# The routing's small tiles in a PSUM bank, and the output rows' positions worked out one step per half step

## The chip, the cores and the metric

The kernel runs on one core of one Trainium2 chip. The metric is the device time of one execution in microseconds; lower is better. Before the change the median of three runs is 992.59 us (992.57 to 993.57). A core has five engines with queues of their own, each served in order: TensorE (PE, its weight loads PEld), VectorE (DVE), ScalarE (ACT), GpSimd (POOL) and SyncE (SP), which here only issues DMAs. SBUF is the memory that all of them reach, PSUM the memory of eight banks that TensorE writes and that VectorE and ScalarE read and write.

## The reference, cut to what matters

Three parts follow each other: an attention with a threshold, a mixture of experts with one expert per token, and a dense layer with a gate. The kernel computes all three in one launch.

```python
scores = scale * q @ k.T; scores = where(scores >= max - tau, scores, -1e9)
x = softmax(scores) @ v                       # 4 x 8 heads x 576 x 64 -> 2304 tokens x 512
logits = x @ w_gate + modality_bias[modality_id]
e_idx = argmax(logits, 1); gate_w = softmax(logits)[e_idx]
for e in range(8):                            # each token through its own expert
    out[e_idx == e] = gate_w * (relu(x[e_idx == e] @ w1[e]) @ w2[e])
h = out @ w_in                                # 512 -> 2048
y = (h * tanh(softplus(h))) @ w_out           # 2048 -> 512
```

## The kernel before, in words

**Attention** goes over 16 pairs of heads in 80 units, TensorE scoring, VectorE and ScalarE masking and exponentiating. When the tokens of a batch are done, `gate` computes their logits and the chosen expert as a one-hot tile `oh`. After half of the tokens, `route_a` (L780) finds the largest expert and gathers the rows of the first item, so that the expert stage can start before the routing is done.

**The expert stage** works in items of 512 rows (`W`) that belong to one expert: five in the straight part (NST), the last one of 288 rows. An item has 8 steps (NF), one for each 128 columns of the hidden layer; n counts the steps over all items, 40 in all. Step n loads the weights of step n + 2 (`load_step`, SP queue), splits weights into a high and a low half (`w_split`, ScalarE and GpSimd, L937 and L938, tiles w0h, w0l, w1h, w1l), runs the up pass of 12 matmuls, splits its relu into hh (ScalarE, L956) and hl (VectorE, L957), and runs the down pass of step n - 1, which needs the hh and hl of that step. From n = 9 (DEC0) on VectorE also decodes the weights of the dense layer (`dec_bits`, L1172 to L1176, a PSUM tile `dect`), one chunk a step and two at some steps (DECB); their loads `dr` (L1164) are issued on the SP queue.

**The routing** proper, `route_b` (L806), runs beside the first item. It is a list of some 90 small steps, nearly all VectorE instructions on tiles of 1 to 240 columns: `ops(1)` (L674) ranks the tokens of the second half within their experts; the lines L826 to L866 compute the experts and the starts of the items (registers `regs`); `place(0)` (L815, L817 to L820) gives every token a position in the items, and `Ids` (L703) turns positions into a list of row numbers `ids_p`, by comparing (at, L735; one-hots qt, L724), marking (ab, L729) and four groups of five small matmuls (L769) whose sum ScalarE copies to `lo` (L775) and VectorE combines (L753). With `ids_p` GpSimd gathers the rows of the second item (`gather_all`, indirect DMAs, L882), which TensorE turns (`x_turn`, L898, eight transposes to a pair of tiles). After that, `rd` does the same for the positions in the output (`place(1)` and a second `Ids`, to `ids_d`), which only the dense layer's stores use, from 688 us on.

**What sets the order.** The engines' queues are written out by the program. `run_bg` (L1205) is called in `half`, twice a step, once before and once after the down pass (h = 2n and 2n + 1). It takes steps off the list `bg` while a planned clock stays below a limit: a small step is planned at 0.19 us (DVC), a step of `Ids` at 0.06 us and more. Pieces with a `pe` part (the small matmuls) are put into TensorE's queue when the plan says that their operands are ready. When `bg` is empty, `half` issues the gather and appends `rd()` to `bg`:

```python
if 1 not in xg and not bg:
    run_pool(99)
    xg[1] = gather_all(ids_p[:, 0:4], xg_p)
    xs[1] = x_new()
    turn_at = next(i for i in range(2 * NF) if i == 2 * NF - 2 or pe_time(i) > clock[0] + DVG)
    bg.extend(rd())
```

At the end of step 8 the list must be empty; the pools of the routing are closed and the first three loads of `dr` issued into their place. All routing tiles lie in SBUF. PSUM is split into two pairs of banks (`ps_s`), a ring of three banks (`ps_t`, `pt_tile`) and one single bank (`ps_a`, `pa_tile`), which attention uses for its results, `x_turn` for every second tile of the second item's rows, and decoding for `dect`.

**The dense layer** follows, with TensorE and VectorE both near full.

Of the kernel before, what the change touches and what calls it, by code (L numbers as in the profile page):

```python
# [25 lines left out]
E = 8  # L26
# [60 lines left out]
def chain_kernel(ctx: ExitStack, tc: tile.TileContext, q, k, v, tau, mid, w_gate, mbias, w1, w2, w_in, w_out, cst, out):  # L87
# [564 lines left out]
    one = C("ones")[:, 0:E * HC]  # L652
# [8 lines left out]
    class Totals(Piece):  # L661
# [8 lines left out]
        def ev(self):  # L670
            nc.scalar.copy(out=pre[self.h], in_=self.t)


    def ops(h, pl):  # L674

        o = oh[:, h]
        of = o.rearrange("p e c -> p (e c)")
        exc, tmp = f("exc", E, HC, pl=pl), f("tmp", E, HC, pl=pl)
        ds, dp, pb = f("ds", HC, pl=pl), f("dp", 2, pl=pl), f("pb", E, pl=pl)
        t2 = f("t2", 2, E, pl=pl)  # L680
        wb = wsw.unsqueeze(2).to_broadcast([P, E, HC])
        excf = exc.rearrange("p e c -> p (e c)")
        return [

            lambda: vec.tensor_tensor(out=t2, in0=pre[h], in1=wsw.unsqueeze(1).to_broadcast([P, 2, E]), op=ALU.mult),
            lambda: vec.tensor_tensor(out=tmp, in0=o, in1=wb, op=ALU.mult),
            lambda: vec.tensor_reduce(out=dp, in_=t2, op=ALU.add, axis=AX.X),
            lambda: vec.tensor_reduce(out=ds, in_=tmp.rearrange("p e c -> p c e"), op=ALU.add, axis=AX.X),
            lambda: vec.tensor_tensor(out=t2, in0=dp.unsqueeze(2).to_broadcast([P, 2, E]),
                                      in1=wsw.unsqueeze(1).to_broadcast([P, 2, E]), op=ALU.mult),  # L690
            lambda: vec.tensor_tensor(out=tmp, in0=ds.unsqueeze(1).to_broadcast([P, E, HC]), in1=wb, op=ALU.mult),
            lambda: vec.tensor_tensor(out=pre[h], in0=pre[h], in1=t2, op=ALU.subtract),
            lambda: vec.tensor_tensor(out=o, in0=o, in1=tmp, op=ALU.subtract),
            lambda: vec.tensor_tensor_scan(out=excf, data0=one, data1=of, initial=0.0, op0=ALU.mult, op1=ALU.add),
            lambda: vec.tensor_tensor(out=exc, in0=exc, in1=o, op=ALU.subtract),
            lambda: vec.tensor_tensor(out=pb, in0=pre[h][:, 0, :], in1=exc[:, :, 0], op=ALU.subtract),
        ] + ([lambda: vec.tensor_tensor(out=pb, in0=pb, in1=pre[0][:, 1, :], op=ALU.add)] if h else []) + [
            lambda: vec.tensor_tensor(out=exc, in0=exc, in1=pb.unsqueeze(2).to_broadcast([P, E, HC]), op=ALU.add),
            lambda: vec.tensor_tensor(out=exc, in0=exc, in1=o, op=ALU.mult),
            lambda: vec.tensor_reduce(out=rank[:, h], in_=exc.rearrange("p e c -> p c e"), op=ALU.add, axis=AX.X),  # L700
        ]

    class Ids:  # L703


        def __init__(self, pos, nc_, nb, ids, pl):
            self.a = (pos, nc_, nb, ids)
            self.pi, self.ai = f("pi", nc_, dt=I32, pl=pl), f("ai", nc_, dt=I32, pl=pl)
            self.af, self.qf = f("af", nc_, pl=pl), f("qf", nc_, pl=pl)
            m, self.qc = (1, HC) if nc_ == HC else (2, HC // 2)  # L710
            self.at = f("at", self.qc, nb, dt=BF16, pl=pl)
            self.ab = [f(f"ab{i}", self.qc, 2, nb, dt=BF16, pl=pl) for i in range(m)]
            self.qt = [f(f"qt{i}", self.qc, P, dt=BF16, pl=pl) for i in range(m)]
            self.lo = f("lo", 2, nb, pl=pl)

        def some(self, c0):
# [4 lines left out]
            qt, ab = (z[c0 // qc % 2] for z in (self.qt, self.ab))  # L721
# [34 lines left out]

    class IdSum(Piece):
# [4 lines left out]
        def pe(self):  # L762
# [4 lines left out]
            qt, ab = (z[c0 // o.qc % 2] for z in (o.qt, o.ab))  # L767
# [12 lines left out]
    def route_a(pl):  # L780
# [18 lines left out]
            *ops(0, pl),  # L799
# [3 lines left out]
            *Ids(pos0, HC, 4, ids_0, pl).steps(),  # L803
        ]

    def route_b(pl):  # L806
        tot, cmp, ni, nis, ist, start, off = (f(n, E, *([NST] if n == "cmp" else []), pl=pl)
                                              for n in ("tot", "cmp", "ni", "nis", "ist", "start", "off"))
        it_e, it_p, i16, fw = f("it_e", NIT, pl=pl), f("it_p", NIT, pl=pl), f("i16", NIT, pl=pl), f("fw", 1, pl=pl)
        it_c, it_d = f("it_c", NIT, E, pl=pl), f("it_d", NIT, E, pl=pl)  # L810
        b0, b0i, wide = f("b0", 1, pl=pl), f("b0i", 1, dt=I32, pl=pl), f("wide", 1, pl=pl)
        sel, pos = f("sel", 2, E, HC, pl=pl), f("pos", 2, 2, HC, pl=pl)
        bi = [P, NIT, E]

        def place(z, base):  # L815
# [3 lines left out]
                    lambda: vec.tensor_reduce(out=pos[:, z], in_=sel.rearrange("p h e c -> p h c e"), op=ALU.add, axis=AX.X),  # L819
                    lambda: vec.tensor_tensor(out=pos[:, z], in0=pos[:, z], in1=rank, op=ALU.add)]  # L820
# [4 lines left out]
            *ops(1, pl),  # L825
            lambda: vec.tensor_tensor(out=tot, in0=pre[0][:, 1, :], in1=pre[1][:, 1, :], op=ALU.add),  # L826
# [4 lines left out]
            lambda: vec.tensor_tensor_scan(out=nis, data0=one[:, 0:E], data1=ni, initial=0.0, op0=ALU.mult, op1=ALU.add),  # L831
            lambda: vec.tensor_tensor_scan(out=start, data0=one[:, 0:E], data1=tot, initial=0.0, op0=ALU.mult, op1=ALU.add),
# [5 lines left out]
            *place(0, ist),  # L838
            lambda: vec.tensor_scalar(out=fw, in0=full, scalar1=-float(W), scalar2=None, op0=ALU.mult),
            lambda: vec.tensor_scalar(out=pos[:, 0], in0=pos[:, 0], scalar1=fw[:, 0:1], scalar2=None, op0=ALU.add),  # L840
# [27 lines left out]
            *Ids(pos[:, 0].rearrange("p h c -> p (h c)"), NC, NBLK, ids_p, pl).steps(),  # L868
        ], lambda: [*place(1, start), *Ids(pos[:, 1].rearrange("p h c -> p (h c)"), NC, NT // P, ids_d[:, 0:NT // P], pl).steps()]
# [28 lines left out]
    def x_turn(xg, x, kd, w=W, single=True):  # L898
        t = (pa_tile("xt") if single and kd % 2 == 0 else pt_tile([P, W], "xt"))[:, 0:w]
# [492 lines left out]
    def half(h):  # L1392
# [9 lines left out]
        if 1 not in xg and not bg:  # L1402
# [4 lines left out]
            bg.extend(rd())  # L1407
# [13 lines left out]
    for n in range(NS + 1):  # L1421
# [22 lines left out]
        half(2 * n)  # L1444
        if n > 0:
# [23 lines left out]
        if 4 <= g < 4 + KD and 0 < it < NST - 1:  # L1469
            x_turn(xg[it + 1], xs[it + 1], g - 4, width(it + 1), n < DEC0)  # L1470
# [11 lines left out]
    assert dp > len(dec)  # L1482
# [111 lines left out]
```

## Time and profile before

| | |
|---|---|
| median of 3 runs | 992.59 us (992.57 to 993.57) |
| the profiled execution | 996.13 us, its span 994.3 us, mean granted clock 0.988 |
| busy: TensorE | 930.9 us (94%) |
| busy: VectorE | 815.8 us (82%) |
| busy: GpSimd | 665.5 us (67%) |
| busy: ScalarE | 519.7 us (52%) |

The span runs from the first to the last instruction of the profiled execution, and all times in the rows count from its start. The expert stage lies at about 349 to 597 us, its first item at 349 to 415, its second at 415 to 462. A row of an instruction has its start, its duration, and in brackets the idle time of its engine before it and what ended it. A duration includes time in which an instruction has started and can't go on. Matmuls are pipelined, so that their rows overlap and the spacing of their starts is their pace. The granted clock is a share of TensorE's upper level.

### The profile page before, as it was taken

The page shows a single profiled execution, that of the slowest core. Times are in us where ns is not written, and L with a number is a line of the kernel's source. Part 1 is how long each engine was busy: PE and PEld are TensorE (multiplying, and loading weights), DVE is VectorE, ACT ScalarE, POOL GpSimd, SP SyncE. Part 2 cuts the span into 40 slices and gives each one's busy share as a digit, 9 for nine tenths or more (in the row PEclk, how much of TensorE's full clock was granted, in tenths as well). Part 3 has the DMA queues.
Part 4 walks back from the last instruction along what each step waited for, and adds up shares of the span by engine and source line. Part 5 has one row for each costly group of instructions (what it writes and reads, how often), then busy time and mean ns, then how long its engine had stood idle before and what let it go on. Part 6 is the DMA issues. An engine that isn't in the chain of part 4 may idle for free. (4 is left out here: it accounts for less than half of the span.)

```text
span 994.3 us, 17630 instructions
## 1 busy us (share of the span) xinstructions
PE 930.9 (94%) x6157; PEld 783.2 (79%) x6157; DVE 815.8 (82%) x1116; ACT 519.7 (52%) x1044; POOL 665.5 (67%) x771
## 2 busy tenths in 40 slices
PE   8899989998979997899999799999999999999994
PEld 5788888788868776688887788888888888888983
DVE  5677786687957768978876579999999999999992
ACT  4577777776768732366654643434344333433341
POOL 4354564455556364577876786887887888787883
PEclk9899999999999999999999999999999999999998
DMA  7678766646567053498899849010001100000000
GB/s 173 138 176 232 190 174 154 143 116 153 136 165 171 7 181 96 134 333 264 257 323 314 292 165 335 1 43 22 22 1 43 43 1 22 11 33 1 1 32 34
DMA packets 120526, 127.47 MB, mean 128 GB/s; under 512 B 54576, under 2 KB 83504, under 8 KB 119920
## 3 DMA queue, kind: packets, MB, share of 16 engines
q1 hardware_dynamic: 117472, 116.58, 40.8%
q0 software_dynamic: 2960, 9.70, 2.9%
q8 instruction: 51, 0.84, 0.3%
q14 instruction: 43, 0.35, 0.1%
HBM read 71.66 MB, written 27.33 MB: 100 GB/s over the span
## 5 line engine op out<-in xcount | busy, mean ns | idle before, releaser
L1298 DVE RECIPROCAL v<-v 128x512 f32<-128x512 f32 (+1 forms) x73 | 241.6, 3309 | 2.5
L373 DVE TENSOR_REDUCE mn<-s 128x1 f32<-128x576 f32 x144 | 106.3, 750 | 61.4 <-PE s L362 36.0
L381 ACT ACTIVATE e<-s,mn 128x576 f32<-128x576 f32 x144 | 105.1, 741 | 88.8 <-DVE mn L373 82.3
L379 POOL TENSOR_SCALAR th<-mn,taus 128x1 f32<-128x1 f32 x140 | 40.5, 290 | 147.5 <-DVE mn L373 134.5
L1292 POOL TENSOR_TENSOR u<-u,v 128x512 f32<-128x512 f32 (+1 forms) x73 | 93.1, 1276 | 64.4 <-ACT v L1291 63.0
L391 DVE SCALAR_TENSOR_TENSOR p<-s,th,e 128x576 f32<-128x576 f32 x144 | 115.2, 815 | 21.2 <-ACT e L381 9.3
L944 PE MATMUL h<-ybh,wil 128*128 128x512 f32 (+1 forms) x320 | 117.7, 368 | 0.0
L942 PE MATMUL h<-ybh,wih 128*128 128x512 f32 (+1 forms) x320 | 117.7, 368 | 0.0
L943 PE MATMUL h<-ybl,wih 128*128 128x512 f32 (+1 forms) x320 | 117.7, 368 | 0.0
L1321 PE MATMUL o<-wo,gh 128*128 128x512 f32 x288 | 112.8, 392 | 1.9 <-ACT gh L1305 1.5
L1297 DVE TENSOR_SCALAR v<-u 128x512 f32<-128x512 f32 (+1 forms) x73 | 109.5, 1500 | 5.6 <-POOL u L1292 3.7
L1323 PE MATMUL o<-wo,gl 128*128 128x512 f32 x288 | 112.7, 391 | 0.3
L1322 PE MATMUL o<-wo,gh 128*128 128x512 f32 x288 | 112.7, 391 | 0.0
L1289 ACT ACTIVATE u<-h 128x512 f32<-128x512 f32 (+1 forms) x73 | 43.2, 592 | 128.6 <-PE h L944 126.0
L1307 POOL TENSOR_TENSOR gl<-v,gh 128x512 fp32r<-128x512 f32 (+1 forms) x73 | 105.7, 1448 | 0.3 <-ACT gh L1305 0.3
L1305 ACT CAST gh<-v 128x512 fp32r<-128x512 f32 (+1 forms) x73 | 44.9, 615 | 111.3 <-DVE v L1303 111.3
L1299 POOL TENSOR_TENSOR u<-u,v 128x512 f32<-128x512 f32 (+1 forms) x73 | 93.3, 1278 | 7.7 <-DVE v L1298 7.7
L361 PE MATMUL s<-xkh,xq 128*128 128x288 f32 x248 | 81.2, 342 | 12.1 <-DVE p L391 10.1
L429 PE MATMUL av<-pt,mv 128*64 128x128 f32 (+1 forms) x1280 | 82.8, 272 | 0.0
L938 POOL TENSOR_TENSOR w0l<-w1r,w0h 128x512 fp32r<-128x512 f32 x39 | 50.7, 1300 | 47.4 <-ACT w0h L937 34.3
L401 PE MATMUL tp<-zident,p 128*128 128x128 f32 x576 | 79.3, 275 | 0.7 <-DVE p L391 0.4
L416 ACT COPY pt<-tp 128x512 f32<-128x512 f32 x144 | 78.4, 598 | 0.4 <-PE tp L401 0.4
(251 smaller groups left out, 2337.9 us busy)
## 6 DMA issues: line engine op xcount, KB each, us to landing
w1r<-in_moe_w SPq DMA_DIRECT2D x40, 256.0 KB
w2r<-in_moe_w SPq DMA_DIRECT2D x40, 256.0 KB
xkh<-hik SPq DMA_DIRECT2D x64, 144.0 KB
xkl<-lok SPq DMA_DIRECT2D x64, 144.0 KB
dr<-in_moe_w_in SPq DMA_DIRECT2D x16, 512.0 KB
dr<-in_moe_w_out SPq DMA_DIRECT2D x16, 512.0 KB
wo<-wo_d SPq DMA_DIRECT2D x14, 512.0 KB
y_d<-zero SPq DMA_DIRECT2D x8, 576.0 KB
```

The lines of the kernel that those rows point to most:

```text
L373: nc.vector.tensor_reduce(out=mn[:, x:x + 1], in_=r["s"][:, :, 0:HK], op=ALU.min, axis=AX.XY)
L381: nc.scalar.activation(out=r["e"], in_=r["s"][:, :, 0:HK], func=AF.Exp, scale=-1.0, bias=res[i, j, 0]["mn"][:, x:x + 1])
L391: nc.vector.scalar_tensor_tensor(out=p, in0=r["s"][:, :, 0:HK], scalar=res[i, j, 0]["th"][:, x:x + 1], in1=r["e"], op0=ALU.is_le, op1=ALU. ...
L942: nc.tensor.matmul(o, lhsT=wh, rhs=xh, start=first, stop=False)
L943: nc.tensor.matmul(o, lhsT=wh, rhs=xl, start=False, stop=False)
L944: nc.tensor.matmul(o, lhsT=wl, rhs=xh, start=False, stop=last)
L1297: nc.vector.tensor_scalar(out=v_, in0=u, scalar1=WTOP, scalar2=2.0, op0=ALU.min, op1=ALU.add)
L1298: nc.vector.reciprocal(out=v_, in_=v_)
L1307: nc.gpsimd.tensor_tensor(out=l, in0=v_, in1=t.bitcast(F32), op=ALU.subtract)
L1321: nc.tensor.matmul(o, lhsT=gh[:, sl], rhs=wo[0, f_], start=f_ == 0, stop=False)
L1322: nc.tensor.matmul(o, lhsT=gh[:, sl], rhs=wo[1, f_], start=False, stop=False)
L1323: nc.tensor.matmul(o, lhsT=gl[:, sl], rhs=wo[0, f_], start=False, stop=f_ == NFO - 1)
```

## The change

The tiles of `route_b` go into the single PSUM bank, so that each VectorE operation of it has one operand, or its result, there. A class `Bank` hands out columns of that bank. `wsw` is copied there by ScalarE (`wsp`), a tile of ones is set there, intermediate tiles (tmp, exc, pb, t2, the corrected totals, pos, it_c, it_e, and of `Ids` pi, ai, af, qf, at) lie there and others stay in SBUF, so that no operation has both inputs in SBUF; `it_p` is computed twice, once for each place; `fw` moves to ScalarE; only the second half of the row sums is copied to `lo`, the first is read from PSUM. `route_a` keeps its tiles in SBUF.

`rd` is no longer appended to `bg`. Its tiles lie in SBUF in a pool of their own, its `Ids` has one group of 20 columns in place of four of 5, and `later()` takes one of its 24 steps after each half of the steps n = 10 to 21. The pools of the other routing tiles are closed at the end of step 8 as before. `x_turn` takes all its tiles from the ring of three.

```diff
+    class Bank:
+        def __init__(self, t):
+            self.t, self.n = t, 0
+        def part(self, *shape, at=None):
...
+            v = self.t[:, o:o + m]
...
         def ev(self):
             nc.scalar.copy(out=pre[self.h], in_=self.t)
+            if self.h:
+                nc.scalar.copy(out=wsp, in_=wsw)
...
+    def ops(h, pl, wsw, one, bank=None):
...
+        exs, ds, dp = f("exc", E, HC, pl=pl), f("ds", HC, pl=pl), f("dp", 2, pl=pl)
+        if bank:
+            tmp, exc, pb, t2, po = (bank.part(*z) for z in ((E, HC), (E, HC), (E,), (2, E), (2, E)))
+        else:
+            tmp, exc, pb, t2, po = f("tmp", E, HC, pl=pl), exs, f("pb", E, pl=pl), f("t2", 2, E, pl=pl), pre[h]
...
-            lambda: vec.tensor_tensor(out=pre[h], in0=pre[h], in1=t2, op=ALU.subtract),
+            lambda: vec.tensor_tensor(out=po, in0=pre[h], in1=t2, op=ALU.subtract),
...
-            lambda: vec.tensor_tensor(out=exc, in0=exc, in1=o, op=ALU.subtract),
-            lambda: vec.tensor_tensor(out=pb, in0=pre[h][:, 0, :], in1=exc[:, :, 0], op=ALU.subtract),
+            lambda: vec.tensor_tensor(out=exs, in0=exc, in1=o, op=ALU.subtract),
+            lambda: vec.tensor_tensor(out=pb, in0=po[:, 0, :], in1=exs[:, :, 0], op=ALU.subtract),
...
+            if bank:
+                self.pi, self.ai = bank.part(nc_).bitcast(I32), bank.part(nc_).bitcast(I32)
+                self.af, self.qf = bank.part(nc_, at=0), bank.part(nc_, at=nc_)
+                self.at = bank.part(qc, nb, at=2 * nc_)
...
-                lambda: vec.scalar_tensor_tensor(out=ids, in0=self.lo[:, 0, :], scalar=64.0, in1=self.lo[:, 1, :],
+                lambda: vec.scalar_tensor_tensor(out=ids, in0=self.t[:, 0:nb], scalar=64.0, in1=self.lo,
...
-                nc.scalar.copy(out=o.lo.rearrange("p a b -> p (a b)"), in_=o.t)
+                nc.scalar.copy(out=o.lo, in_=o.t[:, o.a[2]:])
...
+    def route_b(pl, late, bank):
+        nonlocal wsp
+        n0 = 200
+        wsp, one = bank.part(E, at=n0), bank.part(96, at=n0 + E)
+        block = ops(1, pl, wsp, one[:, 0:E * HC], bank)
...
+        vec.memset(one, 1.0)
+        it_c = one.rearrange("p (a b) -> p a b", b=E)
+        tot, ni, ist = (bank.part(E) for _ in range(3))
...
+        ids = Ids(pos.rearrange("p h c -> p (h c)"), NC, NBLK, ids_p, pl, HC // 2, bank)
+        ids1 = Ids(pos1.rearrange("p h c -> p (h c)"), NC, NT // P, ids_d[:, 0:NT // P], late, NC)
...
-            lambda: vec.tensor_scalar(out=fw, in0=full, scalar1=-float(W), scalar2=None, op0=ALU.mult),
-            lambda: vec.tensor_scalar(out=pos[:, 0], in0=pos[:, 0], scalar1=fw[:, 0:1], scalar2=None, op0=ALU.add),
+            lambda: nc.scalar.activation(out=fw, in_=full, func=AF.Copy, scale=-float(W)),
+            lambda: vec.tensor_scalar(out=pos, in0=pos, scalar1=fw[:, 0:1], scalar2=None, op0=ALU.add),
...
-            lambda: vec.tensor_scalar(out=it_p, in0=it_p, scalar1=float(NT), scalar2=None, op0=ALU.min),
-            lambda: vec.tensor_copy(out=regs[:, NIT:2 * NIT], in_=it_p),
+            lambda: vec.tensor_scalar(out=it_q, in0=it_f, scalar1=float(NT), scalar2=None, op0=ALU.min),
+            lambda: vec.tensor_copy(out=regs[:, NIT:2 * NIT], in_=it_q),
+            lambda: vec.tensor_scalar(out=it_p, in0=it_f, scalar1=float(NT), scalar2=None, op0=ALU.min),
...
-        ], lambda: [*place(1, start), *Ids(...).steps()]
+            *ids.steps(),
+        ], [*place(pos1, start, sel1), *ids1.steps()]
...
-    def x_turn(xg, x, kd, w=W, single=True):
-        t = (pa_tile("xt") if single and kd % 2 == 0 else pt_tile([P, W], "xt"))[:, 0:w]
+    def x_turn(xg, x, kd, w=W):
+        t = pt_tile([P, W], "xt")[:, 0:w]
...
+    rb, rd = route_b(rt, rd_p, Bank(pa_tile("route")))
     bg += gt + rb
...
-            bg.extend(rd())
+
+    def later():
+
+        x = rd.pop(0)
+        if hasattr(x, "pe"):
+            x.pe()
+            x.ev()
+        else:
+            (x[1] if isinstance(x, tuple) else x)()
...
         half(2 * n)
+        if n > DEC0 and rd:
+            later()
...
         half(2 * n + 1)
+        if n > DEC0 and rd:
+            later()
...
-            td.close()
+            t1.close()
             tg.close()
             de_p = pool(td, "de", DEB)
```

## Rows read from the trace of the kernel before

**Rows 1.** Busy time by stretch: us; PE, PEld, DVE, ACT, POOL busy; clock; DMA; GB/s.

```profile
375.70:384.30 8.60, 4.49 (x14) 3.10 (x13) 8.12 (x31) 1.14 (x3) 2.54 (x2) 0.80 0.35 114
396.50:417.70 21.20, 17.70 (x101) 14.07 (x100) 20.53 (x42) 7.14 (x13) 10.15 (x10) 1.00 0.34 98
421.00:486.00 65.00, 64.77 (x296) 53.27 (x295) 52.10 (x79) 39.85 (x72) 53.60 (x45) 1.00 0.90 300
```

**Rows 2.** Waits of TensorE, 348 to 418 us: total, times, longest.

```profile
PE y L943 <- DVE hl L957: 4.1, 1, 4.1
PE pid L769 <- DVE ab L729: 3.7, 3, 2.5
```

**Rows 3.** VectorE in order of time: start us, us, engine, line, operation.

```profile
362.11 1.18 DVE L685 TENSOR_TENSOR t<-pre,wsw 128x16 f32<-128x16 f32 x1 [0.20 <-ACT pre L671]
...
371.69 1.11 DVE L820 TENSOR_TENSOR pos<-pos,rank 128x20 f32<-128x20 f32 x1
...
377.34 1.20 DVE L849 TENSOR_TENSOR it_c<-it_c,off 128x96 f32<-128x96 f32 x1
...
379.46 0.68 DVE L957 SCALAR_TENSOR_TENSOR hl<-h,hh 128x512 fp32r<-128x512 f32 x1
```

**Rows 4.** GpSimd in order of time.

```profile
371.48 1.29 POOL L938 TENSOR_TENSOR w0l<-w1r,w0h 128x512 fp32r<-128x512 f32 x1 [3.41 <-ACT w0h L937]
```

**Rows 5.** ScalarE in order of time.

```profile
371.77 0.59 ACT L956 ACTIVATE hh<-h 128x512 fp32r<-128x512 f32 x1
```

**Rows 6.** Groups of VectorE by form (395:520, 540:590, 362:393): busy us, mean ns.

```profile
L957 DVE SCALAR_TENSOR_TENSOR hl<-h,hh 128x512 fp32r<-128x512 f32 x21 | 14.3, 683 | 5.3 <-ACT hh L956 4.1 <-issue 1.1
...
L957 DVE SCALAR_TENSOR_TENSOR hl<-h,hh 128x288 fp32r<-128x288 f32 x8 | 3.5, 439 | 9.4 <-ACT hh L956 9.4
...
L827 DVE TENSOR_TENSOR cmp<-tot,cs 128x40 f32<-128x40 f32 x1 | 0.2, 199 | 0.0
```

**Rows 7.** TensorE in order of time.

```profile
380.20 0.79 PE L943 MATMUL y<-hl,w1h 128*128 128x512 f32 x1 [4.11 <-DVE hl L957]
...
383.33 0.39 PE L944 MATMUL y<-hh,w1l 128*128 128x512 f32 x1
383.55 0.39 PE L942 MATMUL y<-hh,w1h 128*128 128x512 f32 x1
```

**Rows 8.** Waits of the SyncE queue, 400 to 421 us.

```profile
SPq L1164 <- DVE ab L729: 11.0, 1, 11.0
```

**Rows 9.** VectorE in order of time, the placing of the output rows.

```profile
397.46 5.67 DVE L820 TENSOR_TENSOR pos<-pos,rank 128x20 f32<-128x20 f32 x1
...
408.71 0.95 DVE L724 TENSOR_TENSOR qt<-qf,cs 128x256 bf16<-128x256 f32 x3
...
411.11 1.00 DVE L735 TENSOR_TENSOR at<-af,cs 128x90 bf16<-128x90 f32 x1
412.03 2.04 DVE L724 TENSOR_TENSOR qt<-qf,cs 128x256 bf16<-128x256 f32 x3
...
416.57 1.10 DVE L753 SCALAR_TENSOR_TENSOR ids_d<-lo 128x18 int32<-128x18 f32 x1
```

**Rows 10.** GpSimd in order of time, the same stretch.

```profile
401.82 1.26 POOL L938 TENSOR_TENSOR w1l<-w2r,w1h 128x512 fp32r<-128x512 f32 x1
```

**Rows 11.** Waits of VectorE, 421 to 486 us.

```profile
DVE dec L1176 <- ACT dec L1170: 7.6, 4, 3.9
DVE xl L905 <- ACT xh L904: 1.2, 1, 1.2
DVE hl L957 <- ACT hh L956: 1.1, 1, 1.1
DVE yo L974 <- PE y L944: 0.7, 1, 0.7
```

**Rows 12.** ScalarE and VectorE in order of time around 420 us.

```profile
419.12 0.58 ACT L956 ACTIVATE hh<-h 128x512 fp32r<-128x512 f32 x1
...
421.41 0.68 DVE L957 SCALAR_TENSOR_TENSOR hl<-h,hh 128x512 fp32r<-128x512 f32 x1
```

More of the change, by code (lines that the diff above doesn't have):

```diff
@@ L651, in chain_kernel @@
     wsw, xid, full = f("wsw", E), f("xid", E), f("full", 1)
-    one = C("ones")[:, 0:E * HC]
     rank = f("rank", 2, HC)
@@ L703, in chain_kernel, with __init__ @@
     class Ids:
-        def __init__(self, pos, nc_, nb, ids, pl):
+        def __init__(self, pos, nc_, nb, ids, pl, qc, bank=None):
             self.a = (pos, nc_, nb, ids)
[L708 to L714, printed above, removed]
+            self.qc, self.m = qc, min(2, nc_ // qc)
+            if bank:
[3 more added lines that the diff above has]
+            else:
+                self.pi, self.ai = f("pi", nc_, dt=I32, pl=pl), f("ai", nc_, dt=I32, pl=pl)
+                self.af, self.qf = f("af", nc_, pl=pl), f("qf", nc_, pl=pl)
+                self.at = f("at", qc, nb, dt=BF16, pl=pl)
+            self.lo = f("lo", nb, pl=pl)
+            self.ab = [f(f"ab{i}", qc, 2, nb, dt=BF16, pl=pl) for i in range(self.m)]
+            self.qt = [f(f"qt{i}", qc, P, dt=BF16, pl=pl) for i in range(self.m)]
         def some(self, c0):
@@ L720, in some @@
             bc = [P, qc, nb]
-            qt, ab = (z[c0 // qc % 2] for z in (self.qt, self.ab))
+            qt, ab = (z[c0 // qc % self.m] for z in (self.qt, self.ab))
             def qhot(s0, s1):
@@ L766, in pe @@
                 o.t = pt_tile([P, 2 * nb], "pid")
-            qt, ab = (z[c0 // o.qc % 2] for z in (o.qt, o.ab))
+            qt, ab = (z[c0 // o.qc % o.m] for z in (o.qt, o.ab))
             for c in range(o.qc):
@@ L802, in route_a, with place @@
             lambda: vec.tensor_tensor(out=pos0, in0=pos0, in1=rank[:, 0], op=ALU.add),
-            *Ids(pos0, HC, 4, ids_0, pl).steps(),
+            *Ids(pos0, HC, 4, ids_0, pl, HC).steps(),
         ]
[L806 to L812, printed above, removed]
+    def route_b(pl, late, bank):
[3 more added lines that the diff above has]
+        block = ops(1, pl, wsp, one[:, 0:E * HC], bank)
+        assert bank.n == n0
+        bank.n += E + 96
+        vec.memset(one, 1.0)
+        it_c = one.rearrange("p (a b) -> p a b", b=E)
+        tot, ni, ist = (bank.part(E) for _ in range(3))
+        cmp = bank.part(E, NST)
+        it_e, it_f, it_q, i16 = (bank.part(NIT) for _ in range(4))
+        pos = bank.part(2, HC)
+        b0, out_w = bank.part(1), bank.part(1)
+        b0i = bank.part(1).bitcast(I32)
+        nis, off, it_p = f("nis", E, pl=pl), f("off", E, pl=pl), f("it_p", NIT, pl=pl)
+        it_d, fw, wide, sel = f("it_d", NIT, E, pl=pl), f("fw", 1, pl=pl), f("wide", 1, pl=pl), f("sel", 2, E, HC, pl=pl)
+        start, pos1 = f("start", E, pl=late), f("pos1", 2, HC, pl=late)
+        sel1 = f("sel1", 2, E, HC, pl=late)
         bi = [P, NIT, E]
-        def place(z, base):
+        ids = Ids(pos.rearrange("p h c -> p (h c)"), NC, NBLK, ids_p, pl, HC // 2, bank)
+        ids1 = Ids(pos1.rearrange("p h c -> p (h c)"), NC, NT // P, ids_d[:, 0:NT // P], late, NC)
+        def place(pos, base, sel):
             bb = base.unsqueeze(2).to_broadcast([P, E, HC])
@@ L824, in route_b @@
             Totals(1),
-            *ops(1, pl),
-            lambda: vec.tensor_tensor(out=tot, in0=pre[0][:, 1, :], in1=pre[1][:, 1, :], op=ALU.add),
+            *block,
+            lambda: vec.tensor_tensor(out=tot, in0=pre[0][:, 1, :], in1=totals[1], op=ALU.add),
             lambda: vec.tensor_tensor(
@@ L830, in route_b @@
             lambda: vec.tensor_reduce(out=ni, in_=cmp, op=ALU.add, axis=AX.X),
-            lambda: vec.tensor_tensor_scan(out=nis, data0=one[:, 0:E], data1=ni, initial=0.0, op0=ALU.mult, op1=ALU.add),
-            lambda: vec.tensor_tensor_scan(out=start, data0=one[:, 0:E], data1=tot, initial=0.0, op0=ALU.mult, op1=ALU.add),
+            lambda: vec.tensor_tensor_scan(out=nis, data0=C("ones")[:, 0:E], data1=ni, initial=0.0, op0=ALU.mult, op1=ALU.add),
+            lambda: vec.tensor_tensor_scan(out=start, data0=C("ones")[:, 0:E], data1=tot, initial=0.0, op0=ALU.mult, op1=ALU.add),
             lambda: vec.tensor_tensor(out=ist, in0=nis, in1=ni, op=ALU.subtract),
@@ L1481, in chain_kernel @@
                 second.rec(n2 - 1)
-    assert dp > len(dec)
+    assert dp > len(dec) and not rd
     y_store()
```

48 lines of the change are left out of this document (27 added, 21 removed).

## The prediction

> **What bounds it now.** I looked first at the busy time by stretch [rows 1]. From 421 us, in the expert stage's second item, TensorE computes 64.77 us of 65: there the kernel is bound by TensorE, and a microsecond that TensorE loses or gains earlier is carried to the end. Just before, it is not bound so: in 375.7 to 384.3 us TensorE is busy 4.49 us of 8.6 at a mean granted clock of 0.80, and VectorE 8.12. The waits of TensorE in the first item say for whom [rows 2]: once 4.1 us for hl (the low half of the relu, L957), and 3.7 us in three pieces for ab (L729), an operand of the matmuls that sum the row numbers. Both are VectorE's. The third view is VectorE's order of time [rows 3]: the routing's small instructions, some 0.2 us each, stand in its queue ahead of hl, and eight of them take 1.1 to 1.3 us, the first at 362.11, the last at 377.34. GpSimd's order of time beside it shows why [rows 3, 4]: L820 starts at 371.69 while w0l runs on GpSimd from 371.48 to 372.77, and ends at 372.80. The eight read SBUF alone and end as a GpSimd instruction ends. So hl, whose other input from ScalarE was ready at 372.4 [rows 5], started at 379.46.
>
> **Part 1, one operand in PSUM.** What says that such an operand avoids the wait is [rows 6]: L957 reads h from PSUM, and its 21 instructions between 395 and 520 us have a mean of 683 ns, though GpSimd is busy 53.6 us of the 65 from 421 us on (82%) [rows 1]; its narrower form is shorter by 244 ns for 224 columns, so little but columns is in that mean. So I take the waits of the eight as gone: 8 x (1.2 - 0.2) = 8 us earlier for everything behind them. hl would come up in VectorE's queue at 379.5 - 8 = 371.5 and run at 372.4, when ScalarE's half is there. That is what is late next, and it is hidden: TensorE wants hl at about 376, since it stood still for 4.1 us before the matmul at 380.20 [rows 2, 7]. So the 4.1 us go. With them goes what followed: the eight matmuls that start from 380.20 to 383.33 take 3.1 us [rows 7], rows of 0.79 falling to 0.39 us; at the pace after (0.22 us apart) they take 1.8. [...] The waits for ab: 2.5 us of the 3.7 are behind L820 of the second placing (part 2), which moves away; the other 1.2 are chunks of the first placing, which VectorE then reaches 8 us earlier. All 3.7 go. Sum: 4.1 + 1.3 + 3.7 = 9.1 us. Its ends: 10 if the short gaps around these go as well, 6 if the last chunk (VectorE computes it right behind a later hl, so TensorE meets it with little to spare) and half of the 2.5 stay.
>
> The added instructions: one memset of 96 columns, before the first hl, while VectorE waits; a copy of wsw on ScalarE that the first routing instruction now waits for (below 0.2 us by L827's 199 ns [rows 6]); one more minimum; fw on ScalarE, behind a relu half, needed much later. All stand ahead of hl by less than the 3.5 us between 372.4 and 376, so nothing on the path. The price of a PSUM operand: the two forms of L957 give 244/224 = 1.09 ns a column, hence 683 - 512 x 1.09 = 125 ns beyond its columns, and L827, in SBUF alone, has 199 - 40 x 1.09 = 155 [rows 6]. So I take nothing; the ends are -0.03 and +0.03 us each, some 2 us either way over 70 instructions, covered the same way. The turning of the second item's rows now takes all four tiles from the ring of three; a tile comes back when ScalarE and VectorE have read it, some 2 us later, with a down pass of 2.7 us between the pairs: nothing, at most 0.5 us.
>
> [...]
>
> **Part 2, the second placing in steps.** It stood at 396.5 to 417.7 us; now 24 steps stand one per half step from n = 10 to 21, that is in 421 to 486 us of the old trace, all in SBUF. Nothing else moves with it but its 20 small matmuls and one ScalarE copy (same count, 0.5 us, no difference). On SyncE the loads of dr stood 11.0 us for this ab [rows 8]; they now issue earlier. TensorE waited for none of them, so 0, between 0 and -1. GpSimd's queue is passed by nothing. With `dr` issued earlier the DMAs before 421 us get denser; the weights come two steps ahead, so 0 too.
>
> Their own time: 10 one-hots at 0.95/3 = 0.32 [rows 9] make 3.2 us; three instructions of 360 columns at 0.125 + 360 x 0.00109 = 0.52, 1.5; placing, casts and the last, 10 at 0.2, 2.0: 6.7 us. Their waits for GpSimd aren't in the trace at this place. At the old place, the same work lost [rows 9]: L820 5.67 - 0.2 = 5.5, L735 1.00 - 0.2 = 0.8, L724 2.04 - 0.95 = 1.1, L753 1.10 - 0.2 = 0.9: 8.3 us, with GpSimd busy 10.15 of 21.2 us (48%) [rows 1]. The new place has it busy 82%, 1.7 times as much: 14 us. L820 is one odd row: it outlasted four GpSimd instructions up to 403.08 [rows 10], while the others ended with the one they met. With L820 at 1.0 the loss is 3.8, scaled 6.5. I take the middle, 10, and keep 6.5 and 14; from nothing to 21 instructions times 1.29 = 27 us are the outer bounds.
>
> [...]
>
> The cover: between 421 and 486 VectorE waits 10.6 us (7.6 + 1.2 + 1.1 + 0.7) [rows 11], which steps can fill, and hl at the start of it runs 1.7 us after ScalarE's half is done (421.41 against 419.70) [rows 12], which part 1 takes away: 12.3 us of room. Steps beyond it push hl back, decoding stands in the same queue, and TensorE then waits for hl: 6.7 + 10 - 12.3 = 4.4 us lost. With waits of 6.5 it is 0.9, with 14 it is 8.4.
>
> **Sum.** -9.1 + 4.4 = -4.7 us. The profiled execution took 996.13 us for a span of 994.3, so I expect a span of 989.6; its time is 3.5 above the median 992.59, to which I apply the difference: 987.9 us.
>
> **Rivals.**
> (a) The steps find cover (waits of 6.5 or less, or each hl has spare time): a gain of 8 to 10, 982.6 to 984.6 us. For it: TensorE waited for no hl in 421 to 486. Against: GpSimd's 82%. Chance 0.25.
> (b) Slower. At n = 10 to 21 VectorE becomes the bound. Each of the 21 instructions waits out the better part of a GpSimd instruction because a new one always runs. The loss eats up the gain when the waits reach 12.3 + 9.1 - 6.7 = 14.7 us, 0.7 us each; from there it is slower. With 19 us (0.9 each) the loss is 6.7 + 19 - 12.3 = 13.4 and the time 992.6 - 9.1 + 13.4 = 996.9. For it: L820's 5.67 us. Against: 82% of half a 1.29 us instruction is 0.53 us on average, 11 us for the 21. Chance 0.12.
> (c) The two cancel (waits of 13 to 16 us): 991 to 994 us. Chance 0.12.
> [...] Chance 0.05. [...]
> (e) The change doesn't do what it says: small instructions with a PSUM operand still wait. Then only the moved L820's 2.5 us go, and 4.4 come: +1.9, 994.5 us. Against it: L957's mean. Chance 0.04.
> The forecast, 985 to 990.5 us, has 0.42.
>
> **Numbers.** Likeliest 987.9. About 0.2% (2 us) is what a measurement of this kernel can tell from no change: faster means below 990.6, slower above 994.6. Faster: the forecast, (a) and a quarter of (c): 0.42 + 0.25 + 0.03 = 0.70. Same: the rest of (c), (d) and half of (e): 0.09 + 0.05 + 0.02 = 0.16. Slower: (b) and half of (e): 0.14. The range 982 to 994 leaves out most of (b) and the edges of (a) and (e), 2 in 10 at most; without the rivals it would be 985 to 990.5.
>
> **What would show it.** Right: no VectorE instruction of the routing above 0.5 us before the first gather; no TensorE wait for hl and none for ab in the first item; clock 1.00 throughout; the second item's first up pass some 9 us nearer to the first item's. Then in the second item rows of L817 to L820, L724 and L729 of up to 1.3 us and more, and waits of TensorE for hl of some 4 us together between n = 15 and 22. Wrong: routing instructions that still end with GpSimd's, (e); waits for hl near 0, (a), or above 9, (b); longer rows of each small instruction, (d).

## The result, and the profile after

The changed kernel takes 999.47 us (median of 5 runs, 998.18 to 1002.29), beside 993.57 us for the kernel before on the same chip (992.57 to 996.34). The ratio is 1.0061, interval 1.0042 to 1.0081: slower by about 6 us. The forecast was 987.9, its range 982 to 994.

The profiled execution took 998.2 us for a span of 996.4. The first part came as predicted. VectorE in order of time, the rows that answer to [rows 3], and L869, which answers to L827 in [rows 6]:

```profile
360.57 0.18 DVE L708 TENSOR_TENSOR route<-pre,route 128x16 f32<-128x16 f32 x1 [0.28 <-ACT route L672]
...
364.50 0.21 DVE L869 TENSOR_TENSOR route<-route,cs 128x40 f32<-128x40 f32 x1
...
367.72 0.19 DVE L862 TENSOR_TENSOR route<-route,rank 128x20 f32<-128x20 f32 x1
...
369.59 0.26 DVE L891 TENSOR_TENSOR route<-route,off 128x96 f32<-128x96 f32 x1
...
371.13 0.68 DVE L1000 SCALAR_TENSOR_TENSOR hl<-h,hh 128x512 fp32r<-128x512 f32 x1
```

The instructions of 1.1 to 1.2 us are at 0.18 to 0.26, and the fourth hl runs at 371.13 where it ran at 379.46. All the waits of TensorE from 348 to 418 us, which answer to [rows 2]:

```profile
PE pr L666 <- DVE rtot L806: 1.3, 1, 1.3
PE pid L797 <- DVE ab L757: 1.1, 1, 1.1
PE h L987 <- POOL w0l L981: 0.9, 1, 0.9
```

No wait for hl is left, and one of three for ab. How far the first item gained is read from ScalarE's copy of its result and from the first up matmul. The first two rows are of the kernel before, the last two of the changed one:

```profile
348.58 0.50 PE L942 MATMUL h<-xh,w0h 128*128 128x512 f32 x1
...
414.05 1.02 ACT L972 COPY yo<-y 128x1024 f32<-128x1024 f32 x1 [1.02 <-PE y L944]
```

```profile
346.54 0.50 PE L985 MATMUL h<-xh,w0h 128*128 128x512 f32 x1
...
402.88 1.01 ACT L1015 COPY yo<-y 128x1024 f32<-128x1024 f32 x1 [0.76 <-PE y L987]
```

That is 65.47 us before and 56.34 after: 9.1 us gained. From there to the first matmul of the dense layer's down pass it goes the other way. Before and after:

```profile
597.68 0.39 PE L1321 MATMUL o<-wo,gh 128*128 128x512 f32 x1
```

```profile
599.74 0.39 PE L1366 MATMUL o<-wo,gh 128*128 128x512 f32 x1
```

597.68 - 414.05 = 183.63 us before, 599.74 - 402.88 = 196.86 after: 13.2 us lost. The busy time in the first and the last stretch of [rows 1], now in the changed kernel (PE, PEld, DVE, ACT, POOL busy; clock; DMA; GB/s):

```profile
375.70:384.30 8.60, 7.53 (x44) 5.66 (x43) 7.95 (x24) 1.22 (x2) 2.09 (x2) 1.00 0.43 124
...
421.00:486.00 65.00, 58.48 (x269) 45.80 (x269) 62.58 (x89) 33.81 (x61) 46.69 (x37) 0.97 0.70 219
```

The first has the clock at 1.00 and TensorE fuller than before. In the last TensorE falls from 64.77 to 58.48 us, and VectorE rises from 52.10 to 62.58 of 65: VectorE is the bound there now. All waits of TensorE from 402 to 530 us are for what VectorE hands over, or for ScalarE's halves (hh, wih) that stand in ScalarE's queue behind a decode of VectorE:

```profile
PE y L986 <- DVE hl L1000: 2.8, 2, 1.4
PE h L985 <- DVE hl L1000: 2.7, 1, 2.7
PE y L985 <- ACT hh L999: 1.7, 1, 1.7
PE h L986 <- DVE xl L948: 1.4, 1, 1.4
PE h L985 <- ACT wih L1230: 0.5, 1, 0.5
```

These are 9.1 us. The kernel before has 0.2 us of waits from 414 to 530. Over the whole of the two stretches that are compared here, TensorE's idle time explains only half of the 13.2 us: 7.0 us before, 13.9 after. The other half is busy time, 176.6 before and 183.0 after. Most of that is TensorE's clock. It is granted at 0.50 in three stretches of 3.4 us, where the kernel before has 1.00 from 414 to 598 us:

```profile
477.90:481.30 3.40, 3.40 (x10) 2.64 (x9) 3.23 (x5) 0.55 (x2) 2.34 (x2) 0.50 0.36 135
491.60:495.00 3.40, 3.40 (x8) 2.70 (x9) 3.22 (x5) 0.50 (x1) 2.49 (x2) 0.50 0.68 217
570.10:573.50 3.40, 2.94 (x12) 2.94 (x13) 0.00 (x0) 0.13 (x1) 3.40 (x4) 0.50 0.81 257
```

The first two stand right behind waits for VectorE, of 1.7 us up to 475.5, 1.4 up to 477.4, and 2.7 up to 491.5. The third stands at a wait of 2.8 us for GpSimd in the last item, which the kernel before has too, there without the lower clock. In the first two the matmuls of 512 columns start 0.43 us apart, and 0.23 once the clock is back at 1.00. At about half the pace 3.4 us cost some 1.7, so the three cost some 5 us (an estimate from these rows).

The rows account for 13.2 - 9.1 = 4.1 us of the 5.9 between the medians. The profiled executions themselves differ by 2.1, since the changed kernel's came 2.0 us earlier to its first up matmul (346.54 against 348.58), for which the record shows no cause. The 1.8 us left lie inside the spread of either kernel's runs (some 4 us).

VectorE's time by groups, 405 to 500 us, the longest of the second placing's steps (count, busy us, mean ns):

```profile
L752 DVE TENSOR_TENSOR qt<-qf,cs 128x256 bf16<-128x256 f32 x10 | 12.2, 1248 | 0.0
L859 DVE TENSOR_TENSOR sel<-oh,start 128x80 f32<-128x80 f32 x1 | 5.9, 5928 | 0.0
L757 DVE TENSOR_TENSOR ab<-at,cs 128x360 bf16<-128x360 bf16 x2 | 2.1, 1076 | 0.0
```

With ten others, of 0.2 to 1.2 us, the steps hold VectorE for 25.2 us, of which 7.2 are their own time (the sum of the same operations where they never wait, in the fourth experiment). So they wait 18.0 us. VectorE at the longest single one, at one of the others, and at the longest pair; then GpSimd beside them:

```profile
413.63 5.93 DVE L859 TENSOR_TENSOR sel<-oh,start 128x80 f32<-128x80 f32 x1
...
431.97 1.22 DVE L776 TENSOR_SCALAR ai<-pi 128x20 int32<-128x20 int32 x1
...
464.21 6.70 DVE L752 TENSOR_TENSOR qt<-qf,cs 128x256 bf16<-128x256 f32 x2
```

```profile
410.96 0.94 POOL L925 DMA_INDIRECT xg<-x_d,ids_p  x1 [0.30 <-DMA w1r<-in_moe_w]
411.91 1.31 POOL L981 TENSOR_TENSOR w0l<-w1r,w0h 128x512 fp32r<-128x512 f32 x1
...
418.16 1.29 POOL L1231 TENSOR_TENSOR wil<-dec,wih 128x512 fp32r<-128x512 f32 x1
...
431.86 1.29 POOL L981 TENSOR_TENSOR w1l<-w2r,w1h 128x512 fp32r<-128x512 f32 x1
433.11 1.29 POOL L1231 TENSOR_TENSOR wil<-dec,wih 128x512 fp32r<-128x512 f32 x1
```

At n = 10 GpSimd issues the gather of the next item for some 4.7 us, and splits pile up behind it. Six then run without a gap, from 411.91 to 419.45. L859 starts in the second of them, at 413.63, and ends at 419.56, when the run ends. The next gather is at n = 18, and two one-hots there take 6.70 us together, 5.26 the first. These two places make 11.6 of the 18.0 us. The others waited for no more than the one GpSimd instruction that they met, most of them though the next followed without a gap: L776 ended at 433.19, with the split of 431.86 to 433.15, while the next ran from 433.11.

### The profile page after: what moved, and what is told of

Read it like the earlier page. It is cut to its first block, busy times and chain, and to the rows that moved or that the text cites. A ratio compares the mean times of both kernels' runs of the same rounds, so it can differ in the third digit from the quotient of the medians.

```text
span 996.4 us, 17621 instructions
## 1 busy us (share of the span) xinstructions
PE 935.1 (94%) x6157; PEld 785.4 (79%) x6157; DVE 815.0 (82%) x1106; ACT 518.8 (52%) x1046; POOL 667.2 (67%) x771
## 4 chain that ended last, share of the span: by engine, by line
PE 59%; DVE 16%; DMA 6%; POOL 5%; issue 5%; SPq 4%; ACT 3%; POOLq 0%; DVEq 0%; ACTq 0%
PE h L985 8%; PE h L987 8%; PE h L986 8%; PE o L1366 6%; PE o L1367 6%; PE o L1368 6%; DMA mq<-in_q 4%; SPq L310 3%; DVE mn L373 3%; PE av L429 2%; PE s L361 2%; DVE qt L752 2%; DVE p L391 2%; PE y L985 2%; PE y L987 2%
```

## The experiments

All ratios are to the kernel before in the same session; 0.001 is about 1 us. An interval of a difference of two ratios is some 0.003 either way (an estimate from the table's intervals). A kernel "without the 24 steps" writes the output rows in a fixed order. The theory was: the 9 us are real and come from the operand in PSUM; the loss is waiting for GpSimd, above all in the two steps that meet the run of splits behind a gather.

| kernel | median, us | ratio | interval |
|---|---|---|---|
| the change | 999.47 | 1.0061 | 1.0042 to 1.0081 |
| 1 without the 24 steps | 983.79 | 0.9893 | 0.9872 to 0.9913 |
| 2 no step where GpSimd gathers | 991.46 | 0.9974 | 0.9956 to 0.9991 |
| 3 second placing back, in SBUF | 990.63 | 0.9957 | 0.9939 to 0.9975 |
| 4 second placing back, in the bank | 985.63 | 0.9910 | 0.9891 to 0.9928 |
| 5 as 1, two operations, both inputs SBUF | 986.56 | 0.9935 | 0.9912 to 0.9957 |
| 6 as 5, one input in PSUM | 983.15 | 0.9887 | 0.9856 to 0.9918 |
| 7 as 5, two steps later | 983.75 | 0.9905 | 0.9878 to 0.9933 |
| 8 as 5, a single SBUF input | 984.69 | 0.9914 | 0.9888 to 0.9939 |
| 9 as 4, the bank in SBUF | 994.45 | 1.0011 | 0.9993 to 1.0029 |
| 10 as 1, 24 operations that can't wait | 986.70 | 0.9920 | 0.9893 to 0.9947 |
| 11 as 10, with the two of 5 | 990.39 | 0.9957 | 0.9939 to 0.9975 |
| 12 as 1, 24 operations, both inputs SBUF | 1001.99 | 1.0089 | 1.0057 to 1.0120 |

**1. Without the steps.**

```diff
-        ], [*place(pos1, start, sel1), *ids1.steps()]
+        ], []
```

> Leaves out the output rows' positions: the 24 steps are gone, and a fixed order of rows stands in their place (two small VectorE operations during the attention), so rows of the output go elsewhere; all the rest is the changed kernel. Theory (the gain of part 1, about 9 us up to the end of the first item, is real, and everything lost after 404 us is lost behind the steps): 993.6 - 9.2 = 984.4, between 982 and 987. Rival (what is lost after 404 us has another cause that the change also moved, such as the transposes' ring or the earlier decode loads): 992 or more, since 9 to 13 us would be lost again without any step.

983.79 us, as the theory has it. All that was lost after the first item goes with the steps; the transposes' ring and the earlier loads cost nothing that shows.

**2. No step in the expert steps of the gathers.**

```diff
-        if n > DEC0 and rd:
+        if n > DEC0 and rd and g != 2:
```

> The changed kernel, but no step is issued in the expert steps in which GpSimd gathers (the third of each item), so the 24 steps end two expert steps later. Theory (the loss stands on the two steps that were issued as GpSimd began a gather and then ran on without a pause, 5.93 us and the longer of two in 6.70 us): those two waits of 5.7 and 6.2 us go, most of them on the path, 988 to 992, and no VectorE instruction of this stretch waits over 2 us. Rival (many waits of about 1 us each and the steps' own 6.7 us carry the loss): 996 to 999.

991.46 us, some 9 us under the change, half of the loss. The rest stays; the ratio is 0.008 above the kernel without steps. The edit moves every step, so more than the two long waits changed: the steps hold VectorE for 13.9 us in place of 25.2. L859 runs one expert step after the gather's, at 419.67, in what is left of the run behind the gather, and the ten one-hots take 7.8 us instead of 12.2:

```profile
L752 DVE TENSOR_TENSOR qt<-qf,cs 128x256 bf16<-128x256 f32 x10 | 7.8, 815 | 0.0
...
L859 DVE TENSOR_TENSOR sel<-oh,start 128x80 f32<-128x80 f32 x1 | 1.8, 1758 | 0.0
```

**3 and 4. The second placing back at the end of the first item**, with its tiles in SBUF (3) or in the same bank (4). The first two lines of the edit are in both, the others in 4 alone.

```diff
+            bg.extend(rd)
+            rd.clear()
...
+        start_p, again = bank.part(E, at=480), Bank(bank.t)
+        again.n = bank.n - 2 * NC
+        ids1 = Ids(pos.rearrange("p h c -> p (h c)"), NC, NT // P, ids_d[:, 0:NT // P], late, NC, again)
...
+        ], [lambda: vec.tensor_tensor(out=start_p, in0=start0, in1=tot, op=ALU.subtract),
+            *place(pos, start_p, sel1), *ids1.steps()]
```

> Part 1 alone: the small tiles stay in the PSUM bank, the second placing goes back to the end of the first item, one piece behind another as in the kernel before, its tiles in SBUF. Theory: the 9 us of part 1 stay, and the second placing waits there for GpSimd as it did before (5.67, 2.04 and some of about 1 us), partly on the path because the room is smaller now: 985 to 990. Rival (part 1 gains nothing by itself, its 9 us were those of the second placing taken out of the first item): 993 or more.

> Part 1, and the second placing back at the end of the first item with its small tiles in the same PSUM bank, one operand of each operation there. Theory (only operations whose inputs all lie in SBUF wait for GpSimd): no operation of the second placing over 1 us, its own 7 us lie in the room before the second item, 982 to 987, at least 2 us under the one with SBUF tiles. Rival (the room at the first item's end isn't enough for 24 operations, whatever their operands): 989 or more, within 2 us of the one with SBUF tiles.

990.63 and 985.63 us: 5 us apart, and the second is the best complete kernel of this study, 0.9910 of the one before. In SBUF, VectorE at the placing, and then GpSimd:

```profile
389.83 0.23 DVE L859 TENSOR_TENSOR sel<-oh,start 128x80 f32<-128x80 f32 x1
...
390.74 5.62 DVE L862 TENSOR_TENSOR pos<-pos,rank 128x20 f32<-128x20 f32 x1
396.40 0.18 DVE L775 CAST pi<-pos 128x20 int32<-128x20 f32 x1
...
397.56 3.44 DVE L752 TENSOR_TENSOR qt<-qf,cs 128x256 bf16<-128x256 f32 x10
```

```profile
389.11 0.95 POOL L925 DMA_INDIRECT xg<-x_d,ids_p  x1 [0.30 <-issue]
...
391.33 1.27 POOL L981 TENSOR_TENSOR w0l<-w1r,w0h 128x512 fp32r<-128x512 f32 x1
...
395.04 1.27 POOL L981 TENSOR_TENSOR w1l<-w2r,w1h 128x512 fp32r<-128x512 f32 x1
```

L862 is held until the fourth split ends, as L820 was before [rows 9, 10], and TensorE waits 3.7 us for the hl behind it. With the bank, VectorE and GpSimd:

```profile
391.34 0.19 DVE L865 TENSOR_TENSOR route<-route,rank 128x20 f32<-128x20 f32 x1
391.56 0.19 DVE L775 CAST route<-route 128x20 int32<-128x20 f32 x1
...
393.24 3.41 DVE L752 TENSOR_TENSOR qt<-route,cs 128x256 bf16<-128x256 f32 x10
```

```profile
391.73 1.27 POOL L985 TENSOR_TENSOR w0l<-w1r,w0h 128x512 fp32r<-128x512 f32 x1
...
395.46 1.28 POOL L985 TENSOR_TENSOR w1l<-w2r,w1h 128x512 fp32r<-128x512 f32 x1
```

The same gather and four splits run beside the placing, and no operation of it waits: 0.19 us (L865) where 5.62 stood.

**5 to 8. One operation by itself.** In the kernel without steps, one operation behind hl at n = 10 and 18. The edit shown is that of 5; 6 takes a tile of ones in PSUM as one input, 7 stands at n = 12 and 20, and 8 multiplies `oh` by a constant.

```diff
+        if n in (10, 18):
+            rd[0]()
...
+        ], [lambda: vec.tensor_tensor(out=sel1[:, 0], in0=oh[:, 0], in1=start.unsqueeze(2).to_broadcast([P, E, HC]), op=ALU.mult)]
```

> The kernel without the 24 steps (a fixed order of output rows), plus a single VectorE operation of 128x80 with both inputs in SBUF (the kind of the first step) behind the hl of expert steps 10 and 18, the two in which GpSimd gathers. Theory (one such operation waits there until GpSimd's unbroken run of splits behind the gather ends, and two of them make most of the loss): the operation takes 4 to 6.5 us each time, and the ratio to the kernel before goes from 0.989 to about 0.996 to 0.999 (7 to 10 us). Rival (only the whole series of steps hurts, a single wait is absorbed): 0.989 to 0.991, under 2 us.

> The same, with one input of the operation in PSUM (8 columns that a VectorE memset fills just ahead of it), at the same two places. Theory: no wait, the operation takes 0.2 to 0.3 us, ratio 0.989 to 0.991, as without it. Rival (it is the place in the queue that costs, not where the operands lie): as with both inputs in SBUF, 0.996 or more.

> The same operation with both inputs in SBUF, but behind the hl of expert steps 12 and 20, two steps after those of the gathers. Theory: GpSimd pauses between its splits there, the operation waits for one split at most (up to 1.5 us), ratio 0.989 to 0.991. Rival (GpSimd still runs without a pause two steps later, or any wait behind hl costs the same): 0.994 or more.

> An operation of 128x80 with a single SBUF input (a product with a constant) behind the hl of expert steps 10 and 18. Theory (it is two SBUF inputs that are held through the whole run; one input waits for one split at most, as the two casts of the changed kernel did, 0.94 and 1.22 us): up to 1.5 us each, ratio 0.989 to 0.992. Rival (any operation with SBUF operands alone is held through the run): 4 to 6.5 us each, 0.996 to 0.999.

Each pair in VectorE's order of time, in the order 5, 6, 8:

```profile
410.81 5.93 DVE L915 TENSOR_TENSOR sel<-oh,start 128x80 f32<-128x80 f32 x1
...
456.68 4.73 DVE L915 TENSOR_TENSOR sel<-oh,start 128x80 f32<-128x80 f32 x1
```

```profile
417.89 0.24 DVE L863 TENSOR_TENSOR sel<-oh,one 128x80 f32<-128x80 f32 x1
```

```profile
414.34 5.89 DVE L915 TENSOR_SCALAR sel<-oh 128x80 f32<-128x80 f32 x1
...
460.19 4.71 DVE L915 TENSOR_SCALAR sel<-oh 128x80 f32<-128x80 f32 x1
```

The operand's place decides how long the operation takes: 0.24 us both times with one input in PSUM, 5.93 and 4.73 with both in SBUF, at the same places and beside the same run of splits. Two expert steps later (7) the first took 0.23 us and the second 0.64. On two points the theory was wrong. A single SBUF input doesn't help, it is held as long (5.89 and 4.71 us). And the two waits cost less alone than expected, 0.9935 - 0.9893 = 0.0042, some 4 us of 10; in 8, held as long, it is 0.0021. The times of 5 to 8 lie too near each other to tell them apart. TensorE's waits from 410 to 540 us do: 1.7 us in 5 and 1.4 in 8, none in 6 and 7.

**9. The bank in SBUF.**

```diff
-    rb, rd = route_b(rt, rd_p, Bank(pa_tile("route")))
+    rb, rd = route_b(rt, rd_p, Bank(rt.tile([P, 512], F32, name="route")))
```

> The kernel with both placings in the bank (the second at the end of the first item), with one edit: the bank is a tile of the same size in SBUF, so every operation, its order and its length stay and only the place of the operand moves. Theory (part 1's gain is the operand in PSUM): the waits of up to 1.2 us per small operation come back in the routing and 5 us or more behind the gather, 993 to 1000, ratio 1.000 to 1.006. Rival (the gain comes from the other arrangement: the shorter third placing loop, the freed ring, the order): 985 to 988, ratio under 0.994.

994.45 us, ratio 1.0011: with the operations and their order kept, moving the tile takes back all of the gain of kernel 4, 0.0101 or 10 us. TensorE waits for hl again, 340 to 420 us: the 4.1 us of before [rows 2] are back as 4.0, and 3.2 more stand behind the held operation of the second placing, where before had 2.5 for ab:

```profile
PE y L990 <- DVE hl L1004: 4.0, 1, 4.0
PE xt L950 <- DVE hl L1004: 3.2, 1, 3.2
```

**10 to 12. Own time, waits, and both.**

```diff
     def later():
+        scr = rd.pop()
+        nc.vector.tensor_scalar(out=scr, in0=ht[:, 0:192], scalar1=0.5, scalar2=None, op0=ALU.mult)
...
+        ], [lambda: vec.tensor_tensor(out=sel1, in0=oh, in1=oh, op=ALU.mult)] * 24
```

The first edit is that of 10 (`ht` is the step's h in PSUM); 11 puts the operation of 5 in two of the places; the last line is that of 12.

> The kernel without the 24 steps (a fixed order of output rows), with 24 VectorE operations in their places that do nothing for the result and never meet GpSimd: each reads 192 columns of the expert step's own PSUM tile and multiplies them by a constant, about 0.27 us, 6.4 us in all, as much as the steps' own time. Theory (what the steps lose is waiting for GpSimd, not their own time): 984 to 986.5, ratio 0.989 to 0.992. Rival (VectorE's queue in the second item has no room for 6 us more): 990 or more, ratio 0.996 or more.

> No real steps (a fixed order of output rows). In their 24 places 22 operations with one input in PSUM (0.35 us each, never held) and, in the first places of expert steps 10 and 18, the two operations with both inputs in SBUF that meet GpSimd's unbroken run. Theory (the room of VectorE in the second item takes either the steps' own time or the two long waits nearly for nothing, 2.7 and 3 to 4 us when each stands alone, but not both, which is why taking the two waits out of the changed kernel gave 8 us): 991 to 996, ratio 0.997 to 1.002, more than the sum. Rival (the costs only add): 989 to 991, ratio 0.995 to 0.9965.

> No real steps (a fixed order of output rows), but in their 24 places one operation each with both inputs in SBUF (128x160, about 0.25 us by itself, 6 us in all); nothing depends on its result, no matmul and no evacuation belongs to it. Theory (operations that wait for GpSimd in these places are the whole loss, whatever they compute): 995 to 1001, ratio 1.001 to 1.007, as the changed kernel. Rival (a good part of the loss is the 20 matmuls of the last placing on TensorE's queue and what waits behind them): 988 to 993, ratio under 0.999.

The operations of 10 as a group (ns: shortest, median, longest):

```profile
L1458 DVE TENSOR_SCALAR scr<-h x24: 348/350/360, 417.4 to 483.2; 128x192 f32<-128x192 f32 x24
```

They took 0.35 us each, 8.4 in all, more than planned, never waited, and cost 0.0027 over kernel 1, which is within the noise. So own time is some 3 us, at most 6, of the 17 that the change lies above kernel 1 (1.0061 - 0.9893), and in the trace no wait of TensorE for VectorE from 410 to 540 us comes with it. In 11 the cost is 0.0064, beside 0.0027 + 0.0042 = 0.0069 if the two only add. The rival came and not the theory's "more than the sum", going by the time. TensorE's waits from 410 to 540 us point the other way (4.4 us in 11, against 0.5 in 10 and 1.7 in 5), so a shared room isn't excluded. In 12 nothing depends on the operations, and the time is at or above that of the change. Its longest rows, the operations of one expert step each:

```profile
416.59 6.37 DVE L915 TENSOR_TENSOR sel<-oh 128x160 f32<-128x160 f32 x2
...
470.31 6.36 DVE L915 TENSOR_TENSOR sel<-oh 128x160 f32<-128x160 f32 x2
```

They hold VectorE for 28.3 us. One that was not held took 0.32, so some 20.6 are waits, more than the 18.0 of the change, and TensorE waits 8.9 us from 410 to 540, beside 9.1. So operations in SBUF at these places suffice for a loss of this size; the matmuls and evacuation of the placing aren't needed to explain it. The 24 real steps with an operand in PSUM were not run at their new place; kernels 6 and 10 stand in for them.

## Why the prediction was wrong

**Part 1 was right.** Predicted 9.1 us with ends 6 and 10, measured 9.1 in the profiled executions. The main reasons held too: the wait of 4.1 us for hl is gone, and so is the slow stretch of [rows 7], with 1.00 in place of 0.80. That it is the operand's place and not the rearrangement is shown by kernel 9. That the sum agrees to 0.1 us is partly luck. A wait for ab of 1.1 us stayed where all 3.7 were taken as gone. TensorE's idle time in the two stretches fell by 6.3 us (9.7 to 3.4), not by 4.1 + 3.7; its busy time fell by 2.8, more than the 1.3 of the prediction (3.1 less 1.8 us [rows 7]; the mean granted clock of the kernel before was 0.55 there, from 380.2 to 383.6), also because small matmuls of the second placing moved out of the stretch (304 matmul rows before, 289 after). The fourth hl was forecast for 371.5 to 372.4 and ran at 371.13, but the changed kernel's profile came to its first up matmul 2.0 us earlier. From the first routing instruction to that hl are 17.35 us before (362.11 to 379.46) and 10.56 after (360.57 to 371.13): VectorE gained 6.8 us there and not 8.

**The price of a PSUM operand was right by the length of the rows, and too low by their pace.** The lengths are 0.21 us for L869 against 0.199 for L827 [rows 6], and 0.19 against 0.18 us for the cast L775 in kernels 4 and 3. But rows overlap. From L775 to the first one-hot, six instructions, kernel 4 takes 1.68 us (391.56 to 393.24) and kernel 3 takes 1.16 (396.40 to 397.56); so does kernel 9, with the bank in SBUF. That is 0.09 us each: in SBUF some of the six start before the one ahead has ended, in the bank none does. Rival (d), with its chance of 0.05, stood for longer rows of each small instruction, and no run shows them beyond 0.01 us; what the runs showed in their place is the pace. At the last ab TensorE waited 1.1 us. Rival (e) is out.

**The step that failed is the term "waits for GpSimd, 10 us".** It measured 18.0, beyond the end of 14. The rival that came is (b), VectorE as the bound, whose mark was 14.7 us of waits; its 996.9 us were for 19. Own time was right (6.7 forecast, 7.2 measured). With 18.0 and 7.2 the prediction's own sum gives 7.2 + 18.0 - 12.3 = 12.9 us, beside the measured 13.2, but that is luck: the sum stands for waits of TensorE, and these are 9.1 us in the second item. Much of the rest is the lower clock behind them, 0.50 in three stretches, which the prediction counted in the first item, at 1.3 us, and left out here.

Why was the term too small? The prediction scaled the old place's waits by GpSimd's busy share, 48 to 82%, and took the middle between L820's 5.67 us as the pattern and as one odd row. Both readings were needed, each at its place. L820 started as the gather was being issued, and was held through the four splits that had piled up behind it. At the new place two of the 24 steps meet such a run, at n = 10 and 18, where the program issues the next gathers: 11.6 us. That could be read from the code (`g == 2`) and [rows 9, 10] without a run. The other steps waited 6.4 us in all, which is the low end of 6.5. An unbroken run alone did not hold an operation: L776 got in between two splits without a gap, after 1.22 us. In all profiles here a small operation of the routing, or one in its place, stood past the end of the instruction that it met 14 times, each time in a run that began right behind a gather. Why it is so there is not shown.

**The term "room, 12.3 us" failed too.** Kernel 2 held VectorE for some 14 us and should have cost 2, but cost 8; kernel 5 held it for 10.7 us and should have cost nothing, but TensorE waited 1.4 us for hl. Kernels 10 and 11 (8.4 us, and 7.7 + 10.7) do not decide: nothing and 6 by the term, 2.7 and 6.4 measured. So idle time of VectorE is no store that is emptied first; that the place ahead of hl or a decode sets the cost is a reading of these rows and not shown by itself. Why the short waits of kernel 2 cost more per microsecond than the two long ones of kernel 5 stays open. How the two, 4 us by themselves, make 9 between the change and kernel 2 is answered in part: the change's profile has two stretches of 3.4 us at a clock of 0.50 from 477 to 495 us, some 3.4 us lost (an estimate, as above), a mean of 0.96 from 420 to 500; those of kernels 2 and 11 have 1.00 there. Kernel 12, as slow as the change, has 0.96 too. That is one profile each.

**The range** left out (b), and the chance of slower, 0.14, was too low. The one row that spoke for it was averaged away. With waits of 18.0 its own formula gives 992.6 - 9.1 + 12.9 = 996.4 us; measured were 999.47.

## What to carry to other kernels

A small VectorE operation whose operands all lie in SBUF can be held by GpSimd: here mostly to the end of the one instruction that it met, 1.1 to 1.3 us in the routing of the kernel before, but right behind a gather to the end of the run of splits that had piled up, 4.7 to 5.9 us. Before such work is moved, look for where GpSimd gathers, not only at its busy share. An operand in PSUM avoided the wait, where a bank was free, for 0.01 us in the length of a row and up to 0.09 us in pace. And count what TensorE loses behind a new wait, not the wait alone. The bank was free only early, and keeping the work there was the best of what was tried: with both placings in the bank at the end of the first item the kernel takes 985.63 us, ratio 0.9910 to the kernel before.

## What the runs showed of the hardware

- Right behind a gather, VectorE's operation in SBUF ended within about 0.1 us of the end of GpSimd's run of back-to-back instructions, whether four of them ran (5.62 us) or the rest of one and four more (5.93 us). One SBUF input or two made no difference (5.89 against 5.93).
- Away from the gathers an operation was let in after the one instruction that it met, though the next followed without a gap (L776: 1.22 us, with three splits in a row).
- A gather's own instruction alone did not hold an operation: in kernel 3, L859 started at 389.83 beside the gather's instruction of 389.11 to 390.06 and took 0.23 us. But L862 stood from 390.74, and the first split started at 391.33. What held it in these 0.6 us, beside the gather's last instruction, is not shown.
- With all operands in SBUF, VectorE started some small instructions before the one ahead had ended; with an operand in PSUM it did not in the rows compared (six instructions in 1.16 against 1.68 us).
